# Routing's parts moved within and between chunks, one-hots by scalar per partition, and the last copies of x on GpSimd, in an mLSTM, mixture-of-experts and MLP kernel

## The chip, the cores and the metric

The kernel runs on one core of a Trainium2 chip. The metric is the device time of one execution in microseconds (us), as the median of some runs. The engines are TensorE (PE; its weight loads are listed as PEld), VectorE (DVE), ScalarE (ACT), GpSimd (POOL) and the queue of SyncE (SP), which issues most of the transfers.

## The reference

Three stages in a row: an mLSTM attention over 768 steps, 2 x 8 heads of 40; a mixture of 8 experts in which each of 1536 tokens takes its two best; and an MLP.

```python
def _attn_ref(q, k, v, i_gate, f_gate, o_gate):
    for t in range(S):
        m_new = np.maximum(f_gate[:, :, t] + m, i_gate[:, :, t])
        f_stab = np.exp(f_gate[:, :, t] + m - m_new)
        i_stab = np.exp(i_gate[:, :, t] - m_new)
        C = f_stab * C + i_stab * einsum('bhd,bhe->bhde', vt, kt)
        n = f_stab * n + i_stab * kt
        y[:, :, t] = o * einsum('bhde,bhe->bhd', C, qt) / max(|n.q|, 1)

def _moe_ref(x, w_gate, w_noise, noise, w1, w2):
    noisy_logits = x @ w_gate + log1p(exp(x @ w_noise)) * noise
    top2 = np.argpartition(-noisy_logits, 2, axis=1)[:, :2]
    top2_w = softmax of the two
    for e in range(E):
        out[mask] += top2_w[mask] * (relu(x[mask] @ w1[e]) @ w2[e])

def _moe2_ref(x, w_in, w_out):
    h = x @ w_in
    return (h * clip(h + 3, 0, 6) / 6) @ w_out
```

## The kernel before

**Attention.** The 768 steps are cut into NT = 12 chunks of 64 for both batches (128 partitions: 2 batches x 64 steps). The loop at L1137 runs chunks n = 0 to 9; chunks 10 and 11 are written out behind it (L1201 to L1228). In a chunk: `pmul(n+1)` (VectorE: scores times decay), `inter(n)` and `values(n)` (TensorE), `logits(n-2)` (TensorE: the router's logits of an earlier chunk), `norm2(n-1)` (ScalarE: the chunk's x, then the copy of its last 64 columns, and SP's store of x into `Xd`), `state(n)` (TensorE, then VectorE's Sb), `norm_eg` and `norm_pv` (VectorE: y, its denominator), `scores(n+2)` and `expo(n+2)` (TensorE, then ScalarE's dd), `xpose(n-1)` (TensorE transposes x, ScalarE copies xT), and parts of the weights' split: `w_load` (SP loads a piece into one of four buffers `raw`), `w_hi` (ScalarE casts its high part) and `w_lo` (VectorE subtracts for the low part). The schedule is by hand: each engine runs its instructions in the order of the program's text.

**Routing.** `route(m)` is a generator for tokens of four chunks (m = 0, 1, 2). Its parts: the logits' copy (L475) and softplus; the two best and one-hots over experts (up to L518); the counting by matmuls on TensorE (L527 to L538); the slot of each token (to L582); one-hots of the slot's low part over 128 columns (LO, L587) and its high part over 32 (H and HV, L592, L595); matmuls that turn these into lists of tokens (L605); `idx` (L608) and the copy of slots (L612); and the shares of the two experts (L617 to L621). Each `yield` ends a step; a `yield` with "D" or "P" ends a part. `go(r)` runs to the next such part; after `fine[0] = True` the function `step()` advances by one `yield` from within the later code, and `until(m)` runs on until list m is found. The logits and lists of all routes, and half of the output of `values`, lie in PSUM bank 7 (`wb`).

**Experts.** `units` are eight experts cut into tiles of up to 416 tokens, with experts 0 and 1 begun on the tokens of the first eight chunks (units 0 and 1) and finished later (units 2 and 8). For each unit `gather` (GpSimd, indirect) fetches tokens from `Xd` by `idx`, `xprep` transposes them on TensorE and ScalarE and VectorE split them into XH and XL; a step f runs `L1` (TensorE, then hb on ScalarE and VectorE), and `L2` two steps later (LAG). `bg(i, f, fn)` puts a piece of other work at step f of unit i, behind its matmuls, `bga` ahead of the L2; WS lists at which steps `w_split` (`w_hi`, `w_lo`, `w_load`) runs.

**MLP.** Units M0 = 9 and later are the MLP. `conv` converts its float64 weights in pieces of six parts on VectorE, ScalarE (L748) and SP; `combine` joins the two experts' rows by the shares.

Of the kernel before, what the change touches and what calls it, by code (L numbers as in the profile page):

```python
# [11 lines left out]
F32 = mybir.dt.float32  # L12
# [13 lines left out]
NT = 12  # L26
# [18 lines left out]
R4 = 4  # L45
XP = (2, 3, 5, 6)
VSPLIT = {}
WS = ((0, 0), (0, 1), (0, 3), (0, 5), (0, 7), (1, 1), (1, 2), (1, 4), (1, 6), (2, 1))
# [24 lines left out]
def mlstm_moe_mlp(ctx, tc, qk, kv, on, gf, gf4, sl, w1, w2, w_in, w_out, cf, cb, out):  # L73
# [329 lines left out]
    def norm2(n):  # L403
# [9 lines left out]
        A.copy(x[:, DM:XW], x[:, 256:DM])  # L413
        xt[n] = x
        nc.sync.dma_start(Xd[n * 128:(n + 1) * 128], x)
# [40 lines left out]
    found, now = [0], [False]  # L456
# [14 lines left out]
    def route(m):  # L471
# [48 lines left out]
        e2 = small([128, R4, 1], "e2")  # L520
# [13 lines left out]
        A.activation(e2, dl, AF.Exp)  # L534
# [46 lines left out]
        lf = small([128, 2, 2 * R4], "lf", F16)  # L581
# [3 lines left out]
        for i in (0, R4):  # L585
            LO.append(scratch(R4, 128))
            V.tensor_tensor(LO[-1], iotab[:, None, :].to_broadcast([128, R4, 128]),  # L587
                            lf[:, 0, i:i + R4, None].to_broadcast([128, R4, 128]), OP.is_equal)
            yield
        hh = wp.tile([128, DM], F32, name="yo2", bufs=1).bitcast(F16)  # L590
        H, HV = [hh[:, i:i + 64 * R4].rearrange("p (j c) -> p j c", c=32) for i in (0, 64 * R4)]
        V.tensor_tensor(H, iotab[:, None, 0:32].to_broadcast([128, 2 * R4, 32]),  # L592
                        lf[:, 1, :, None].to_broadcast([128, 2 * R4, 32]), OP.is_equal)
        yield
        V.tensor_tensor(HV.rearrange("p (n k) c -> p n k c", n=R4), H.rearrange("p (n k) c -> p n k c", n=R4),  # L595
                        tokf[:, tks, None, None].to_broadcast([128, R4, 2, 32]), OP.mult)
# [4 lines left out]
        while fine[0] and spot[0] < at + SPI and not now[0]:  # L601
            yield
        pi = pz[:, 128:160]
# [12 lines left out]
        sm = small([128, R4, 1], "s")  # L616
        V.tensor_scalar(sm, e2, 1.0, 1e-9, OP.add, OP.add)  # L617
        yield
        V.reciprocal(wab[:, :, 0:1], sm)
        yield  # L620
        V.tensor_tensor(wab[:, :, 1:2], wab[:, :, 0:1], e2, OP.mult)  # L621
        yield
# [509 lines left out]
    def norm(n):  # L1132
        norm_pv(n)
        norm2(n)

    L = NT - 3
    for n in range(NT - 2):  # L1137
# [13 lines left out]
        if n in (7, 9):  # L1151
            go(r0)
# [5 lines left out]
        if n > 1:  # L1158
            norm2(n - 1)
        if n and n % 2 == 0:  # L1160
            gate(n, 2)
# [10 lines left out]
        if n >= 5:  # L1172
            go(r0)
# [10 lines left out]
        scores(n + 2)  # L1184
# [248 lines left out]
```

## Time and profile before

| | us |
|---|---|
| median of 3 runs | 508.97 |
| lowest, highest | 506.79, 509.3 |
| the profiled execution | 510.91 |
| its span, first to last instruction | 509.1 |

| engine | busy us | share of the span |
|---|---|---|
| TensorE, matmuls | 478.2 | 94% |
| TensorE, weight loads | 436.5 | 86% |
| VectorE | 332.4 | 65% |
| ScalarE | 238.5 | 47% |
| GpSimd | 96.4 | 19% |

The attention stage runs to about 98 us, the experts to about 324, the MLP to the end. A row of the timeline gives start, duration, engine, line, operation, output and inputs, shape and count; what stands in brackets is how long the engine was idle before it and what ended that. [...] The shares of busy time are means over stages with different limits.

### The profile page before, as it was taken

The numbers are of one execution on the slowest core, as the hardware profiler recorded it, in microseconds if no ns is written. First come the engines' busy times: TensorE is split into PE (matmuls) and PEld (weight loads), VectorE is DVE, ScalarE is ACT, GpSimd is POOL, SyncE is SP. The second block draws the span as 40 slices with busy tenths as digits, with TensorE's granted clock in tenths as the row PEclk, the third lists the DMA queues.
The fourth block names the chain that finished last, engine by engine and source line by source line (L and its number), as shares of the span: only waits on it lengthen the run. The fifth ranks groups of instructions, "written<-read, shape, count | busy, mean of one in ns | idle before, by whom it ended". The sixth has DMA issues, their size and how long they took to land. (4 is left out here: it accounts for less than half of the span.)

```text
span 509.1 us, 11544 instructions
## 1 busy us (share of the span) xinstructions
PE 478.2 (94%) x4554; PEld 436.5 (86%) x4554; DVE 332.4 (65%) x823; ACT 238.5 (47%) x509; POOL 96.4 (19%) x115
## 2 busy tenths in 40 slices
PE   6898887799999999999999999899999999999996
PEld 3676665698899999999999999789888989899985
DVE  4844788588648788887878774577886334353534
ACT  3576568265435454545455633556463324233331
POOL 2322211503231111111110021785101000000000
PEclk9999995599999999999999999999999999999999
DMA  8597672555755798979797696869313400020111
GB/s 208 161 298 188 199 225 102 145 178 169 263 180 193 245 301 273 310 258 312 264 311 245 215 308 196 280 189 327 135 53 108 151 1 1 1 52 1 26 26 52
DMA packets 41192, 91.00 MB, mean 179 GB/s; under 512 B 4816, under 2 KB 23504, under 8 KB 41136
## 3 DMA queue, kind: packets, MB, share of 16 engines
q1 hardware_dynamic: 34736, 69.52, 43.0%
q0 software_dynamic: 5728, 19.73, 12.8%
q10 hardware_dynamic: 672, 0.99, 0.7%
q8 instruction: 36, 0.59, 0.5%
q14 instruction: 20, 0.16, 0.1%
HBM read 67.42 MB, written 22.68 MB: 177 GB/s over the span
## 5 line engine op out<-in xcount | busy, mean ns | idle before, releaser
L952 DVE SCALAR_TENSOR_TENSOR r<-r,bank 128x512 f32<-128x512 f32 (+1 forms) x56 | 34.2, 611 | 82.0 <-ACT r L951 78.9
L951 ACT ACTIVATE r<-bank,cft 128x512 f32<-128x512 f32 (+1 forms) x56 | 35.1, 627 | 96.9 <-PE bank L937 88.3
L940 ACT ACTIVATE hb<-bank 128x416 fp32r<-128x416 f32 (+2 forms) x80 | 35.7, 447 | 88.5 <-PE bank L937 75.6
L937 PE MATMUL bank<-XH,SB 128*128 128x416 f32 (+3 forms) x280 | 75.8, 341 | 0.3 <-PEq L1037 0.3
L937 PE MATMUL bank<-XL,SB 128*128 128x416 f32 (+3 forms) x192 | 67.0, 349 | 0.6 <-DVE XL L876 0.6
L973 PE MATMUL bank<-SB,hb 128*128 128x320 f32 x192 | 61.9, 322 | 2.4 <-ACT hb L924 2.1
L973 PE MATMUL bank<-SA,hb 128*128 128x320 f32 x192 | 60.8, 317 | 0.0
L864 POOL DMA_INDIRECT XG<-Xd,idx x32 | 34.6, 1081 | 138.2 <-PE bank L874 110.2
L975 PE MATMUL bank<-SA,hb 128*128 128x320 f32 x192 | 59.4, 309 | 0.1
L975 PE MATMUL bank<-SB,hb 128*128 128x320 f32 x192 | 59.5, 310 | 0.0
L974 PE MATMUL bank<-SA,hb 128*128 128x320 f32 x192 | 59.2, 308 | 0.0
L974 PE MATMUL bank<-SB,hb 128*128 128x320 f32 x192 | 59.2, 308 | 0.0
L937 PEld LDWEIGHTS bank<-XH,SB 128*128 128x128 f32 x280 | 50.3, 189 | 4.6 <-issue 0.6
L937 PE MATMUL bank<-XH,SA 128*128 128x416 f32 (+2 forms) x200 | 50.9, 327 | 0.0
L973 PEld LDWEIGHTS bank<-SB,hb 128*128 128x128 f32 x192 | 36.2, 188 | 3.9 <-ACT hb L924 2.5
L937 PE MATMUL bank<-XL,SA 128*128 128x416 f32 (+2 forms) x120 | 39.0, 326 | 0.0
L937 PEld LDWEIGHTS bank<-XL,SB 128*128 128x128 f32 x192 | 36.2, 188 | 2.8 <-DVE XL L876 0.8
L937 PEld LDWEIGHTS bank<-XH,SA 128*128 128x128 f32 x200 | 36.2, 194 | 1.4
L973 PEld LDWEIGHTS bank<-SA,hb 128*128 128x128 f32 x192 | 36.1, 188 | 1.1
L974 PEld LDWEIGHTS bank<-SA,hb 128*128 128x128 f32 x192 | 36.2, 188 | 0.9
L974 PEld LDWEIGHTS bank<-SB,hb 128*128 128x128 f32 x192 | 36.2, 189 | 0.6
L975 PEld LDWEIGHTS bank<-SA,hb 128*128 128x128 f32 x192 | 36.0, 188 | 0.6 <-DVE hb L925 0.3
(215 smaller groups left out, 1038.9 us busy)
## 6 DMA issues: line engine op xcount, KB each, us to landing
raw<-in_w_dram SPq DMA_DIRECT2D x18, 640.0 KB
raw<-in_w_dram SPq DMA_DIRECT2D x18, 512.0 KB
craw<-in_w_in_dram SPq DMA_DIRECT2D x8, 640.0 KB
craw<-in_w_out_dram SPq DMA_DIRECT2D x8, 640.0 KB
raw<-in_w_dram SPq DMA_DIRECT2D x18, 256.0 KB
qk<-in_qk_dram SPq DMA_DIRECT2D x23, 192.0 KB
Yd<-yo SPq DMA_DIRECT2D x24, 160.0 KB
kv<-in_kv_dram SPq DMA_DIRECT2D x11, 324.0 KB
```

Of the source, the lines that this page charges most:

```text
L864: G.indirect_dma_start(out=XG[0:n, (u.xo + i) % 4, :], out_offset=None, in_=Xd[0:CUT[u.i] * 128] if early else Xd[:, :], in_offset=bass.In ...
L937: T.matmul(p, a, b, start=(i == 0), stop=(i == 7))
L940: A.activation(hb[:, 0:N], p, AF.Relu)
L951: A.activation(r, p, AF.Relu, bias=three)
L952: V.scalar_tensor_tensor(r, r, 6.0, p, OP.min, OP.mult)
L973: T.matmul(p, h, wh, start=s, stop=False)
L974: T.matmul(p, h, wl, start=False, stop=False)
L975: T.matmul(p, hb[:, lo:lo + n], wh, start=False, stop=t)
```

## The change

The calls `go(r0)` of chunks 5 to 9 go from behind `norm_pv` to the end of the chunk, and the counting of route 0 from ahead of `logits` in chunk 7 to behind `scores`. The one-hots over the slot are made by 16 VectorE instructions, each with one column of `lf` (now float32) as a scalar per partition, in place of three that broadcast and one that multiplies; their `yield`s are two more for LO and one more for HV. The exponential for the shares goes ahead of the list's matmuls. The shares are put aside and run at steps 2, 4 and 6 of unit 1. The store of x is a function of its own, `put`, called behind `norm2`. The copy of x's last 64 columns runs on GpSimd for chunks 10 and 11. One `w_lo` and `w_load` goes from ahead of unit 0 into it; WS has other steps; list 2 and the gather of unit 2 are asked for at step 1 of unit 1, not 2; and `conv` runs at the odd steps of unit M0, not the even ones.

```diff
--- before.py
+++ after.py
@@ -45,7 +45,7 @@
 R4 = 4
 XP = (2, 3, 5, 6)
 VSPLIT = {}
-WS = ((0, 0), (0, 1), (0, 3), (0, 5), (0, 7), (1, 1), (1, 2), (1, 4), (1, 6), (2, 1))
+WS = ((0, 2), (0, 3), (0, 4), (0, 5), (0, 7), (1, 2), (1, 3), (1, 4), (1, 6), (2, 1))
 TROWS = CAP + 11 * 128
 OVB = 22
 OV = OVB * 128
@@ -410,9 +410,11 @@
         else:
             G.tensor_tensor(x[:, 0:DM].rearrange("p (a x d) -> p x a d", a=4, x=2), o.rearrange("p (x a) d -> p x a d", x=2),
                             rd.rearrange("p (x a) -> p x a", x=2)[:, :, :, None].to_broadcast([128, 2, 4, D]), OP.mult)
-        A.copy(x[:, DM:XW], x[:, 256:DM])
+        (A.copy if n < NT - 2 else G.tensor_copy)(x[:, DM:XW], x[:, 256:DM])
         xt[n] = x
-        nc.sync.dma_start(Xd[n * 128:(n + 1) * 128], x)
+
+    def put(n):
+        nc.sync.dma_start(Xd[n * 128:(n + 1) * 128], xt[n])
 
 
     Xd = dram.tile([SLOTS, XW], F32, name="Xd")
@@ -453,7 +455,7 @@
                 r = slice(32 * c, 32 * c + 32)
                 T.matmul(p[r], xT[n][0:w, k, r], wgt[0:w, k, :], start=(k == 0), stop=(k == 2))
 
-    found, now = [0], [False]
+    found, now, shares = [0], [False], []
 
     def until(m):
         now[0] = True
@@ -517,7 +519,7 @@
         dl = small([128, R4, 1], "dl")
         V.tensor_tensor(dl, mx[:, :, 1:2], mx[:, :, 0:1], OP.subtract)
         wab = WAB[:, tks]
-        e2 = small([128, R4, 1], "e2")
+        e2 = small([128, R4, 1], "e2", bufs=3)
         if not fine[0]:
             yield "P"
             assert counted[0] >= m
@@ -531,7 +533,6 @@
                      mk[:, i:i + 1].to_broadcast([128, k, 8]), start=False, stop=False, skip_group_check=True)
         T.matmul(pp.rearrange("p (n e) -> p n e", n=R4), ones, run[:, None, :].to_broadcast([128, R4, 8]),
                  start=False, stop=True, skip_group_check=True)
-        A.activation(e2, dl, AF.Exp)
         cuts = [e for e in range(2) if m == CUT[e] // R4]
         if m == 1 or cuts:
             pc = pz[:, 96:104]
@@ -578,28 +579,29 @@
         yield
         V.scalar_tensor_tensor(lh[:, 1], sli, 7, h1, OP.bitwise_and, OP.bitwise_or)
         yield
-        lf = small([128, 2, 2 * R4], "lf", F16)
+        lf = small([128, 2, 2 * R4], "lf")
         V.tensor_copy(lf, lh)
         yield "D" if not fine[0] else None
         LO = []
-        for i in (0, R4):
-            LO.append(scratch(R4, 128))
-            V.tensor_tensor(LO[-1], iotab[:, None, :].to_broadcast([128, R4, 128]),
-                            lf[:, 0, i:i + R4, None].to_broadcast([128, R4, 128]), OP.is_equal)
-            yield
-        hh = wp.tile([128, DM], F32, name="yo2", bufs=1).bitcast(F16)
-        H, HV = [hh[:, i:i + 64 * R4].rearrange("p (j c) -> p j c", c=32) for i in (0, 64 * R4)]
-        V.tensor_tensor(H, iotab[:, None, 0:32].to_broadcast([128, 2 * R4, 32]),
-                        lf[:, 1, :, None].to_broadcast([128, 2 * R4, 32]), OP.is_equal)
-        yield
-        V.tensor_tensor(HV.rearrange("p (n k) c -> p n k c", n=R4), H.rearrange("p (n k) c -> p n k c", n=R4),
-                        tokf[:, tks, None, None].to_broadcast([128, R4, 2, 32]), OP.mult)
+        for j in range(2 * R4):
+            if j % R4 == 0:
+                LO.append(scratch(R4, 128))
+            V.tensor_scalar(LO[-1][:, j % R4], iotab, lf[:, 0, j:j + 1], None, OP.is_equal)
+            if j % 2:
+                yield
+        HV = wp.tile([128, DM], F32, name="yo2", bufs=1).bitcast(F16)[:, 0:64 * R4].rearrange("p (j c) -> p j c", c=32)
+        for j in range(2 * R4):
+            n = R4 * m + j // 2
+            V.tensor_scalar(HV[:, j], iotab[:, 0:32], lf[:, 1, j:j + 1], tokf[:, n:n + 1], OP.is_equal, OP.mult)
+            if j % 4 == 3:
+                yield
         at = spot[0]
         yield
         if not fine[0]:
             yield "P"
         while fine[0] and spot[0] < at + SPI and not now[0]:
             yield
+        A.activation(e2, dl, AF.Exp)
         pi = pz[:, 128:160]
         for j in range(2 * R4):
             T.matmul(pi, LO[j // R4][:, j % R4], HV[:, j], start=(j == 0), stop=(j == 2 * R4 - 1))
@@ -613,13 +615,14 @@
         elif m == 1:
             V.tensor_tensor(slot, slot, pi, OP.add)
         yield
-        sm = small([128, R4, 1], "s")
-        V.tensor_scalar(sm, e2, 1.0, 1e-9, OP.add, OP.add)
-        yield
-        V.reciprocal(wab[:, :, 0:1], sm)
-        yield
-        V.tensor_tensor(wab[:, :, 1:2], wab[:, :, 0:1], e2, OP.mult)
-        yield
+
+        def share():
+            sm = small([128, R4, 1], "s")
+            V.tensor_scalar(sm, e2, 1.0, 1e-9, OP.add, OP.add)
+            V.reciprocal(wab[:, :, 0:1], sm)
+            V.tensor_tensor(wab[:, :, 1:2], wab[:, :, 0:1], e2, OP.mult)
+
+        shares.append(share)
         if m == NT // R4 - 1:
             at = spot[0]
             while spot[0] < at + SP2:
@@ -1132,6 +1135,8 @@
     def norm(n):
         norm_pv(n)
         norm2(n)
+        if n:
+            put(n)
 
     L = NT - 3
     for n in range(NT - 2):
@@ -1148,7 +1153,7 @@
             load_kv(n + 3)
         if n in (0, 1, 3, 5, 7):
             load_on(n + 2 + n % 2 if n else 2)
-        if n in (7, 9):
+        if n == 9:
             go(r0)
         if n >= 2 and n != L:
             logits(n - 2)
@@ -1157,6 +1162,8 @@
             gens.append(r0)
         if n > 1:
             norm2(n - 1)
+        if n:
+            put(n - 1)
         if n and n % 2 == 0:
             gate(n, 2)
         state(n)
@@ -1169,8 +1176,6 @@
         if n == 1:
             G.tensor_copy(adj, iota8)
             G.tensor_copy(iotab, iota128)
-        if n >= 5:
-            go(r0)
         for _ in range(WD[n] if n < len(WD) else 0):
             w_load()
         if n == 0:
@@ -1182,6 +1187,8 @@
         if n == L - 1:
             xpose(n - 1)
         scores(n + 2)
+        if n == 7:
+            go(r0)
         if n == L - 1:
             logits(n - 1)
             r1 = [route(1), "D"]
@@ -1196,6 +1203,8 @@
             decays(n + 2, n + 6)
         if 1 <= n < L - 1:
             xpose(n - 1)
+        if n >= 5:
+            go(r0)
         w_hi(WH[n] if n < len(WH) else 0)
         w_lo(WL[n] if n < len(WL) else 0)
     n = NT - 2
@@ -1207,6 +1216,7 @@
     xpose(n - 2)
     go(r1)
     norm2(n - 1)
+    put(n - 1)
     state(n)
     logits(n - 2)
     fine[0] = True
@@ -1218,8 +1228,6 @@
     norm(n)
     norm_eg(n + 1)
     norm(n + 1)
-    w_lo()
-    w_load()
     open_psd()
     xprep(units[0], 0, 5)
     xpose(n - 1, 2)
@@ -1270,8 +1278,11 @@
     bga(0, 1, last_route)
     bg(0, 0, gather, units[1])
     bg(0, 1, open_late)
-    bg(0, 0, w_lo)
-    bg(0, 0, w_load)
+    for f in range(2):
+        bg(0, f, w_lo)
+        bg(0, f, w_load)
+    for f in (2, 4, 6):
+        bg(1, f, lambda: shares.pop(0)())
     for f in range(8):
         bg(0, f, step, 6 if f < 4 else 4)
     for f in range(3):
@@ -1279,8 +1290,8 @@
     for i, f, *c in WS:
         for g_ in {'h': (w_hi,), 'l': (w_lo, w_load)}[c[0]] if c else (w_split,):
             bg(i, f, g_)
-    bg(1, 2, until, NT // R4)
-    bg(1, 2, gather, units[2])
+    bg(1, 1, until, NT // R4)
+    bg(1, 1, gather, units[2])
     bg(1, 4, gather, units[3], 0, 1)
     bg(1, 7, gather, units[3], 2, 3)
     for i in range(3, M0 - 1):
@@ -1300,7 +1311,7 @@
     bg(M0 - 2, 3, conv_to, 4)
     bg(M0 - 2, 7, conv_to, 8)
     for f in range(8):
-        bg(M0, 2 * f, conv)
+        bg(M0, 2 * f + 1, conv)
         bg(M0 + 1, f, conv, 2)
     bg(M0, 7, conv_to, 12)
     bg(M0 + 1, 7, conv_to, 16)
```

## Rows read from the trace of the kernel before

**Rows 1.** Windows of 10 us: per engine busy us (instructions), granted clock, DMA share, GB/s.

```profile
80.00:90.00 10.00, 6.25 (x188) 5.50 (x187) 9.32 (x38) 6.59 (x18) 1.81 (x2) 0.50 0.38 142
...
110.00:120.00 10.00, 9.44 (x76) 9.03 (x75) 9.76 (x34) 5.33 (x11) 0.00 (x0) 1.00 0.43 142
...
130.00:140.00 10.00, 10.00 (x81) 9.78 (x79) 6.06 (x23) 4.49 (x9) 1.41 (x2) 1.00 0.73 233
```

**Rows 2.** Timeline of TensorE, `values` (L365): start us, us, engine line op tile shape count.

```profile
39.70 1.07 PE L365 MATMUL bank<-kv,P 64*64 64x41 f32 x32
...
68.47 0.66 PE L365 MATMUL bank<-kv,P 64*64 64x41 f32 x32
...
84.20 1.07 PE L365 MATMUL bank<-kv,P 64*64 64x41 f32 x32
```

**Rows 3.** Timeline, waits of chunks 5 to 9; in brackets idle before and releaser.

```profile
56.47 0.65 PE L454 MATMUL bank<-cft,xT 128*32 128x16 f32 x24 [1.19 <-ACT xT L441]
...
63.84 0.21 ACT L534 ACTIVATE e<-dl 128x4 f32<-128x4 f32 x1 [1.40 <-DVE dl L518]
...
75.80 1.09 PE L365 MATMUL bank<-kv,P 64*64 64x41 f32 x30 [1.24 <-DVE zg L475]
...
77.05 0.69 DVE L317 TENSOR_TENSOR P<-s4p,dd 128x512 f32<-128x512 f32 x1 [1.30 <-ACT dd L305]
...
83.09 0.18 PE L527 MATMUL bank<-mk,cbt 128*128 128x32 bf16 x1 [3.06 <-DVE slot L612]
```

**Rows 4.** Timeline of VectorE: three small operations, the one-hots of route 0, the shares.

```profile
69.88 0.17 DVE L576 TENSOR_SCALAR lh<-SL 128x8 int32<-128x8 int32 x1
...
69.96 0.16 DVE L577 TENSOR_SCALAR h<-SL 128x8 int32<-128x8 int32 x1
...
70.16 0.17 DVE L579 SCALAR_TENSOR_TENSOR lh<-SL,h 128x8 int32<-128x8 int32 x1
...
73.57 1.24 DVE L587 TENSOR_TENSOR yo<-iotab,lf 128x512 f16<-128x512 f16 x2
...
74.73 0.42 DVE L592 TENSOR_TENSOR yo<-iotab,lf 128x256 f16<-128x256 f16 x1
...
75.19 0.42 DVE L595 TENSOR_TENSOR yo<-yo,cft 128x256 f16<-128x256 f16 x1
...
82.95 0.16 DVE L617 TENSOR_SCALAR s<-e 128x4 f32<-128x4 f32 x1
...
83.44 0.15 DVE L542 TENSOR_SCALAR t<-bank 128x1 f32<-128x1 f32 x1
```

**Rows 5.** Timeline around the end of the attention stage, 91 to 99 us.

```profile
91.33 0.73 POOL L411 TENSOR_TENSOR x<-od,rd 128x320 f32<-128x320 f32 x1
...
94.05 1.44 DVE L688 TENSOR_TENSOR SA<-raw,SA 128x1280 fp32r<-128x1280 f32 x1
...
94.28 1.79 POOL L411 TENSOR_TENSOR x<-od,rd 128x320 f32<-128x320 f32 x1 [2.21 <-DVE rd L399]
...
96.10 0.24 ACT L413 COPY x<-x 128x64 f32<-128x64 f32 x1 [3.76 <-POOL x L411]
...
97.05 0.65 PE L454 MATMUL bank<-cft,xT 128*32 128x16 f32 x24 [2.67 <-ACT xT L441]
...
98.19 0.56 PE L937 MATMUL bank<-XH,SA 128*128 128x256 f32 x1
```

**Rows 6.** Timeline of units 0 and 1: a split, and waits.

```profile
101.04 1.48 DVE L688 TENSOR_TENSOR SA<-raw,SA 128x1280 fp32r<-128x1280 f32 x1
...
106.71 1.23 DVE L688 TENSOR_TENSOR SB<-raw,SB 128x1024 fp32r<-128x1024 f32 x1 [1.02 <-ACT SB L687]
...
116.36 0.39 PE L937 MATMUL bank<-XL,SB 128*128 128x256 f32 x1 [0.56 <-DVE XL L876]
...
128.79 0.52 PE L874 MATMUL bank<-cft,XG 128*128 128x128 f32 x3 [1.19 <-DMA XG<-Xd,idx]
```

**Rows 7.** Timeline of TensorE in the transition to unit M0.

```profile
328.17 0.41 PE L973 MATMUL bank<-SB,hb 128*128 128x320 f32 x1 [1.02 <-ACT hb L924]
```

## The prediction

> **What bounds the kernel now.** I read the windows of 10 us first, to see where TensorE is not full: from 130 us on it is busy for 10.00 of 10, so whatever is gained or lost before that is carried to the end, apart from the waits in the transition near 328 us [rows 1, 7]. Every edit but one (the conversion's) lies before 135 us. In 80 to 90 TensorE is busy 6.25 of 10 and VectorE 9.32; in 110 to 120 VectorE is busy 9.76 [rows 1]. So the path runs through VectorE at the end of the attention stage and nearly so in unit 0.
>
> Next the clock. The granted clock reads 1.00 at 40 us and 0.50 at 84 us, but the same 32 matmuls of `values` take 1.07 us in both and 0.66 us at 68 us [rows 2]. [...] The sum below therefore prices the stage at the long durations.
>
> Then the waits in time order. TensorE stands 1.24 us before `values(9)` for VectorE's copy of the logits (L475), and 3.06 us before route 1's counting (L527) for the copy of slots (L612) [rows 3]. In the code neither pair shares data: they share PSUM bank 7 (`wb`), so I read it that a write waits for all earlier reads of the bank in program order. This I use below for the new order.
>
> **Routing's parts at the end of a chunk (n = 5 to 9).** `go(r0)` goes behind `scores`, `expo` and `xpose`. VectorE's order changes only in chunks 8 and 9; ScalarE's and TensorE's change in all.
> Chunk 5: ScalarE no longer stands before the gates, dd(7) and xT(4) until VectorE delivers the logits; TensorE's 1.19 us wait for xT [rows 3] goes. Chunk 7: the counting of route 0 (L527 to L532) now stands behind `scores(9)` and ahead of `expo(9)`. By bank 7 it must wait until VectorE has read y of chunk 7; behind it stand `expo(9)`, and for that dd(9) on ScalarE and the product on VectorE. No row has this wait. It can cost nothing, if VectorE has read by then, and at most the 1.19 us that chunk 5 gained, since with those lost chunk 7 stands as before; I take 1.0, since VectorE was the later of the two in this chunk. ScalarE's wait of 1.40 us for `dl` [rows 3] goes, as the exponential of `dl` moves to the counting's next part, where `dl` is long done. Net at the state update of chunk 8: 0 to 1.2 us gained; I take 0.2.
> Chunk 8: the logits' copy now comes ahead of route 0's one-hots on VectorE. So ScalarE's softplus and dd(10) no longer sit behind them, and the 1.30 us that VectorE waits for dd(10) [rows 3] goes: 1.3. The one-hots themselves stay on VectorE's path ahead of pmul(10).
> Chunk 9: the copy of slots comes behind route 1's counting, so the wait of 3.06 falls. It isn't worth 3.06, because VectorE is the fuller engine; late next is bank 7's next reader, the y of chunk 9. The three operations on the shares (82.95 to 83.44) leave VectorE: 0.5 [rows 4]. They return in unit 1 at steps 2, 4 and 6, beside a full TensorE.
> Sum until route 1's list of tokens: 0.2 + 1.3 + 0.5 = **2.0 us** (1.4, if dd(10) comes 0.4 later than VectorE is ready, to 3.0).
>
> **Copies of x on GpSimd, and w_lo moved.** For chunks 10 and 11 ScalarE's copy of 64 columns stands in ScalarE's queue waiting 3.76 us for GpSimd's x; behind it stand the casts of the gathered tokens and xT(9), and TensorE waits 2.67 us for that [rows 5]. GpSimd's x(11) itself took 1.79 us beside VectorE's split L688 (94.05), against 0.73 us for x(10) [rows 5]. After: ScalarE can cast as soon as the transposes are done. TensorE's wait ended at 97.05, so it began at 94.4; unit 0's first matmul came 1.14 after the logits (98.19) [rows 5], so 95.6 on the old time scale. Late next is VectorE's XL of the second tile, at about the same time, and then the gather's landing. I take **2.2 us** (1.5 to 2.6). GpSimd's two copies cost no more than x itself (0.73) each; they stand ahead of the second gather (needed 15 us later) and of the store of x, so nothing is charged; without that cover 0.3 to 1.5. SP's queue keeps its order: each store (`put`) is issued where it was, and the weight loads stay behind it.
>
> **Splits in unit 0.** Two w_lo (1.48 us each [rows 6]) now come at steps 0 and 1, and splits at steps 2, 3, 4, 5, 7 instead of 0, 1, 3, 5, 7. Between step 1's hb and unit 1's XL VectorE gets one w_lo and one split more: 1.48 + 1.2 = 2.7 us, against idle time there of at least 1.02 [rows 6] which it fills. TensorE waits for XL 0.56 us now [rows 6]; it will wait longer by about 1.1, and is repaid when unit 1's step 1 has no split any more. I take **-0.5** (-2.7 to 0). Weights: every piece of WS is still split at least four steps ahead of its first use and its load, from the same four buffers, asked for four or more steps ahead of its cast; nothing is charged.
>
> **Gather of unit 2 at step 1.** In GpSimd's queue nothing else stands there, so the issue doesn't move by the edit itself; but the split that ran beside it goes to step 2. TensorE's 1.19 us wait for its landing [rows 6] shrinks: **+0.6** (0 to 1.2).
>
> **Conversion at odd steps of unit M0.** TensorE waits 1.02 us at 328 for ScalarE's hb [rows 7]; in the code the conversion's L748 of step 0 stands ahead of it on ScalarE. One step later it stands ahead of the next hb, behind `combine`. From one side the wait goes (+1.0), from the other a second one of its size arises (-1.0). I take **0**.
>
> **One-hots.** Before: from 73.57 to 75.61, 2.04 us for a route [rows 4]. After: eight instructions of 128 columns and eight of 32. None of this form is in the trace. From below: two independent small VectorE instructions start 0.08 apart, so 16 x 0.08 = 1.3. From above: each behind the other, 0.20 for 8 columns and 0.46 for 256 (74.73 to 75.19), so about 0.33 for 128 and 0.22 for 32: 8 x 0.33 + 8 x 0.22 = 4.4 [rows 4]. They don't depend on one another, so I stay near the lower row: 0.12 each, 1.9 us, **+0.2** for the two routes on the path (-4.7 to +1.5; the third lies in unit 0, where VectorE has little room).
> [...]
>
> **Sum.** 2.0 + 2.2 - 0.5 + 0.6 + 0 + 0.2 = 4.5 us. The profiled execution took 510.91 us (span 509.1), so 506.4 by its own time. It lies 1.94 us above the median of the three runs, 508.97; on that scale the forecast is **504.5 us**. A difference of 0.5% (2.5 us) is about what a measurement of this kernel can tell from none.
>
> **Rivals.**
> *VectorE keeps the gain in unit 0.* For: 9.76 of 10 busy there already. Against: it idles 1.02 at 105.7, and TensorE waited only 0.56. Price: -2.7 instead of -0.5 and no shorter gather wait: 4.5 - 2.2 - 0.6 = 1.7, so 507.3.
> *Costly one-hots (slower).* If each waits for the one before, a route pays 4.4 instead of 2.04, three routes 7.1, and 4.3 + 0 - 7.1 = -2.8: 511.8. It decides from a mean of 0.22 us an instruction (2.04 + 4.3/3 over 16: no gain left), and 0.27 makes it slower by over 0.5%. Against: the pair 0.08 apart.
> [...]
> *It doesn't do what it says.* Bank 7 holds the moved counting just as long, and the gathered tile lands too late for ScalarE's freed queue to matter: only the 0.5 us of the shares is left, 508.5.
>
> **How the numbers follow.** Forecast 0.50 (nearly all of it under 506.4), earlier clock or cheap one-hots 0.15, VectorE in unit 0 0.22, no effect 0.05, costly one-hots 0.08. Faster: 0.50 + 0.15 less a little for the forecast's upper edge, 0.64; same 0.28; slower 0.08. The range: with the one-hots at their middle the terms' lower ends sum to -0.6 (1.4 + 1.5 - 2.7 + 0 - 1.0 + 0.2) and their upper ends with cheap one-hots to 9.3 (3.0 + 2.6 + 0 + 1.2 + 1.0 + 1.5). That all meet at one end is unlikely; 500 to 509.5 leaves out the costly one-hots and little else.
>
> **What would show it.** Right: no wait of ScalarE for GpSimd's x; `values(9)` and L527 without their waits; VectorE busy throughout from 75 to the list of tokens, and that list 1.4 to 2.8 us earlier; unit 0's first L1 3.5 to 5 us earlier; sixteen one-hots in about 1.9 us; TensorE's wait before unit 1's first L1 longer than 0.56 and the gather's wait shorter than 1.19. Wrong: one-hots of over 0.2 us each; a new TensorE wait of over 2 us for XL or hb in unit 0; the lead at unit 0's start gone by 130 us; or a new stall in unit M0.

## The result and the profile after

The changed kernel took 503.84 us (median of 4 runs, 502.13 to 504.99) against 509.13 for the kernel before (506.79 to 510.53): a ratio of 0.9898, interval 0.9849 to 0.9947. The forecast was 504.5. Run again on another chip, beside the kernel before, it took 507.58 against 510.85: 0.9948, interval 0.9924 to 0.9971. By these medians the change is worth some 3 to 5 us. The total came out as forecast, but by luck: two large errors in the sum cancelled, as the stretches show.

The profiled execution of the changed kernel took 504.61 us, its span 502.8. Its windows (columns as in [rows 1], which they answer):

```profile
80.00:90.00 10.00, 8.15 (x201) 6.51 (x200) 9.38 (x48) 3.36 (x14) 2.40 (x3) 0.50 0.34 122
...
110.00:120.00 10.00, 7.91 (x59) 6.89 (x59) 9.79 (x39) 3.57 (x7) 0.96 (x1) 1.00 0.48 112
130.00:140.00 10.00, 10.00 (x84) 9.85 (x83) 5.77 (x25) 4.48 (x11) 0.03 (x1) 1.00 0.89 273
```

VectorE is as full as before in both critical windows (9.38, 9.79), TensorE is fuller in 80 to 90 and emptier in 110 to 120, and from 130 us on it is full again. (The changed kernel is some 2 us further on in its work in the first of these windows and 4 to 5 in the second, so equal windows don't hold equal work.)

One pair of profiles doesn't tell a change of 1% from chance, so I set the stretches of all profiles side by side. Marks: Sb(n) is the start of VectorE's Sb of chunk n, "list 1" that of idx of route 1, "unit 0" the first L1, "unit 1, 160" the first L1 of 160 columns. "Changed" are the profiles, those of the experiments below among them, whose code in that stretch is that of the changed kernel: six up to list 1, four to unit 0, three in each of the last two.

| stretch | before, two profiles | changed, lowest to highest (mean) | gain | forecast |
|---|---|---|---|---|
| start to Sb(4) | 42.20, 41.37 | 39.50 to 44.35 (40.95) | 0.8 | 0 |
| Sb(4) to Sb(5) | 8.64, 8.64 | 4.63 to 7.49 (6.53) | 2.1 | 0 |
| Sb(5) to Sb(7) | 14.68, 14.58 | 13.09 to 14.76 (14.00) | 0.6 | 1.2 |
| Sb(7) to Sb(8) | 5.52, 5.86 | 6.95 to 6.96 (6.96) | -1.3 | -1.0 |
| Sb(8) to list 1 | 17.43, 17.43 | 17.70 to 17.72 (17.71) | -0.3 | 2.0 |
| list 1 to unit 0 | 9.72, 8.79 | 6.87 to 6.99 (6.92) | 2.3 | 2.2 |
| unit 0 to unit 1, 160 | 36.00, 36.68 | 35.26 to 35.91 (35.60) | 0.7 | 0.1 |
| from there to the end | 374.91, 373.45 | 373.47 to 376.29 (374.48) | -0.3 | 0 |

A gain is the mean of before less that of changed; before rounding they add up to 4.8 us. Of the 4.4 forecast between Sb(5) and unit 0, the routing's 2.2 turned into a loss of 0.9 (0.63 - 1.27 - 0.28); in its place stand 2.9 us from ahead of Sb(5), where I had expected nothing.

Two rows are weaker than they look. Ahead of Sb(5) the other six experiments have the changed kernel's code too. Over all twelve profiles the first row is 39.50 to 44.42 (mean 41.45) and the second 4.63 to 7.54 (6.76), so their gains are 0.3 and 1.9, and the profile of the third experiment reaches Sb(5) at 50.87 us, no earlier than before (50.84, 50.01). In the last row the chip counts: the four profiles on the chip of the second group take 374.99 to 378.53 there, the other profiles of these kernels 373.03 to 374.01.

Single profiles can mislead here. In the profiled execution route 1's list came 1.65 us earlier than before and unit 0's first L1 4.49 earlier, as the prediction's signs ask; but Sb(5) was already 3.42 earlier.

Where the 2.1 between Sb(4) and Sb(5) lie, the timeline of TensorE shows (start us, us, engine line, count, idle time before and what ended it). The kernel before, in its two profiles:

```profile
44.60 1.13 PE L294 MATMUL s4p<-qk 40*64 40x64 f32 x30 [2.31 <-issue]
```

```profile
43.77 1.13 PE L294 MATMUL s4p<-qk 40*64 40x64 f32 x30 [2.31 <-issue]
```

The changed kernel:

```profile
40.41 1.12 PE L294 MATMUL s4p<-qk 40*64 40x64 f32 x30 [0.39 <-issue]
```

"Issue" is a pause for which the profile shows no cause. It is 2.31 us in both profiles of before and at most 1.21 in the twelve of the changed kernel and the experiments.

Now the routing. The timeline of the changed kernel, chunks 7 to 9 (it answers [rows 3, 4]):

```profile
63.72 0.18 PE L529 MATMUL bank<-mk,cbt 128*128 128x32 bf16 x1 [0.78 <-DVE y L386]
...
71.75 1.38 DVE L589 TENSOR_SCALAR yo<-iotab,lf 128x128 f16<-128x128 f16 x8
73.05 2.04 DVE L595 TENSOR_SCALAR yo<-iotab,lf,cft 128x32 f16<-128x32 f16 x7
73.34 0.73 POOL L310 TENSOR_TENSOR kt<-kv,dd 128x320 f32<-128x320 f32 x1 [2.90 <-ACT dd L305]
74.81 0.48 DVE L595 TENSOR_SCALAR yo<-iotab,lf,cft 128x32 f16<-128x32 f16 x2
75.20 0.68 DVE L317 TENSOR_TENSOR P<-s4p,dd 128x512 f32<-128x512 f32 x1
...
80.07 0.18 PE L529 MATMUL bank<-mk,cbt 128*128 128x32 bf16 x1 [1.82 <-DVE y L386]
83.53 1.38 DVE L589 TENSOR_SCALAR yo<-iotab,lf 128x128 f16<-128x128 f16 x8
84.83 1.67 DVE L595 TENSOR_SCALAR yo<-iotab,lf,cft 128x32 f16<-128x32 f16 x8
```

The rows come from two views that meet at 75 us, so one of route 0's eight instructions of 32 columns stands in both. The one-hots of route 0 take from 71.75 to 75.29, 3.5 us, and those of route 1 from 83.53 to 86.50, 3.0, where four instructions took 2.04 [rows 4]. The product for the next chunk (L317) starts as soon as they end: they are on the path. VectorE no longer waits for dd(10); TensorE's counting now waits for bank 7's reader y (0.78 and 1.82) and not for the slots.

Route 0 takes longer than route 1 because of one instruction, here alone:

```profile
73.24 0.86 DVE L595 TENSOR_SCALAR yo<-iotab,lf,cft 128x32 f16<-128x32 f16 x1
```

The others of its kind took 0.28 us. It ran beside GpSimd's product L310 (73.34 to 74.07). In the kernel before, that product came behind the one-hots of 73.57 to 75.61:

```profile
77.09 0.74 POOL L310 TENSOR_TENSOR kt<-kv,dd 128x320 f32<-128x320 f32 x1 [4.74 <-ACT dd L305]
```

It waits for dd(10), which the new order makes earlier, and so it now falls among the one-hots. The experiments on the one-hots and on the order bear this out: some 0.6 us of route 0's 3.5 are the price of the new order, not of the new instructions.

The end of the stage (it answers [rows 5]) and unit 0 (it answers [rows 6]):

```profile
90.48 0.88 PE L877 MATMUL bank<-cft,XG 128*128 128x128 f32 x3 [1.58 <-DMA XG<-Xd,idx]
91.39 0.48 ACT L878 CAST XH<-bank 128x384 fp32r<-128x384 f32 x1 [5.10 <-PE bank L877]
91.62 0.72 POOL L411 TENSOR_TENSOR x<-od,rd 128x320 f32<-128x320 f32 x1 [0.62 <-PE bank L441]
93.70 0.56 PE L940 MATMUL bank<-XH,SA 128*128 128x256 f32 x1
...
109.36 1.48 DVE L691 TENSOR_TENSOR SB<-raw,SB 128x1280 fp32r<-128x1280 f32 x1
...
111.44 0.41 DVE L879 TENSOR_TENSOR XL<-bank,XH 128x256 fp32r<-128x256 f32 x1
...
111.90 0.39 PE L940 MATMUL bank<-XL,SB 128*128 128x256 f32 x1 [1.52 <-DVE XL L879]
```

ScalarE casts as soon as TensorE has transposed; its wait for GpSimd's x is gone, and the gather's landing ends last (1.58). At unit 1's start TensorE's wait for XL has grown from 0.56 to 1.52 us. The split of 1.48 ahead of XL (109.36) stood there before as well:

```profile
113.82 1.48 DVE L688 TENSOR_TENSOR SB<-raw,SB 128x1280 fp32r<-128x1280 f32 x1
```

### The profile page after: what moved, and what is told of

Its sections match the earlier page's. It is cut to its first block, busy times and chain, and to the rows that moved or that the text cites. A ratio compares the mean times of both kernels' runs of the same rounds, so it can differ in the third digit from the quotient of the medians.

```text
span 502.8 us, 11581 instructions
## 1 busy us (share of the span) xinstructions
PE 478.6 (95%) x4554; PEld 436.6 (87%) x4554; DVE 335.9 (67%) x859; ACT 238.3 (47%) x507; POOL 96.5 (19%) x117
## 5 line engine op out<-in xcount | busy, mean ns | idle before, releaser
L949 DVE SCALAR_TENSOR_TENSOR hb<-bank,hb 128x32 fp32r<-128x32 f32 x64 | 12.0, 187 | 37.7 <-ACT hb L943 37.6
L976 PEld LDWEIGHTS bank<-SA,hb 128*128 128x128 f32 x192 | 36.1, 188 | 1.1
L977 PEld LDWEIGHTS bank<-SA,hb 128*128 128x128 f32 x192 | 36.2, 188 | 0.9
```

The lines of the kernel that those rows point to most:

```text
L949: V.scalar_tensor_tensor(hb[:, N:N + u.tail], p[:, o:N], 0.0, hb[:, o:N], OP.max, OP.subtract)
L976: T.matmul(p, h, wh, start=s, stop=False)
L977: T.matmul(p, h, wl, start=False, stop=False)
```

## The experiments

Each kernel but the kernel before, run once more, differs from the changed one by the edit shown. Medians are compared only among kernels that ran together on one chip: the first four, the next four, the last four (there the kernel before took 507.87, 510.85 and 507.96).

**The one-hots as before.**

```diff
-        lf = small([128, 2, 2 * R4], "lf")
+        lf = small([128, 2, 2 * R4], "lf", F16)
...
-            V.tensor_scalar(LO[-1][:, j % R4], iotab, lf[:, 0, j:j + 1], None, OP.is_equal)
...
-            V.tensor_scalar(HV[:, j], iotab[:, 0:32], lf[:, 1, j:j + 1], tokf[:, n:n + 1], OP.is_equal, OP.mult)
...
+            V.tensor_tensor(LO[-1], iotab[:, None, :].to_broadcast([128, R4, 128]),
+                            lf[:, 0, i:i + R4, None].to_broadcast([128, R4, 128]), OP.is_equal)
...
+        V.tensor_tensor(H, iotab[:, None, 0:32].to_broadcast([128, 2 * R4, 32]),
+                        lf[:, 1, :, None].to_broadcast([128, 2 * R4, 32]), OP.is_equal)
...
+        V.tensor_tensor(HV.rearrange("p (n k) c -> p n k c", n=R4), H.rearrange("p (n k) c -> p n k c", n=R4),
+                        tokf[:, tks, None, None].to_broadcast([128, R4, 2, 32]), OP.mult)
```

> The changed kernel with the one-hots made as before: four instructions that broadcast, in place of 16 with a scalar per partition. Theory (the one-hots' price lies on VectorE's path): in the changed kernel the 16 took 3.5 us for route 0 and 3.0 for route 1, before 2.0 each, so from the cast of lf in route 1 to idx it takes 3.2 us in place of 3.98, and with 0.9 to 1.5 us back per route the time is 1.5 to 3 us under the changed kernel's 503.8, about 501.5. Rival (bank 7 or TensorE sets the list's time, and the dearer one-hots hide): the one-hots shrink to 2.0 us but the time stays within 1 us of 503.8.

```profile
72.27 1.28 DVE L588 TENSOR_TENSOR yo<-iotab,lf 128x512 f16<-128x512 f16 x2
73.47 0.42 DVE L593 TENSOR_TENSOR yo<-iotab,lf 128x256 f16<-128x256 f16 x1
73.86 0.74 POOL L310 TENSOR_TENSOR kt<-kv,dd 128x320 f32<-128x320 f32 x1 [2.90 <-ACT dd L305]
73.92 0.96 DVE L596 TENSOR_TENSOR yo<-yo,cft 128x256 f16<-128x256 f16 x1
...
84.77 0.42 DVE L596 TENSOR_TENSOR yo<-yo,cft 128x256 f16<-128x256 f16 x1
```

In this timeline route 0 takes 72.27 to 74.88, 2.6 us, route 1 2.1. Route 0's last instruction took 0.96 us beside GpSimd's product, which route 1's (0.42) doesn't meet. From Sb(7) to list 1 it takes 22.97 us against 24.65 to 24.67 in six profiles of the changed code: 1.7 us for two routes. From lf of route 1 to its idx it takes 3.22, as expected. The time was 502.93 us, ratio to before 0.9898 (0.9871 to 0.9925). Beside the next kernel but one, which has all 16 instructions and 504.38, that is 1.5 us less; the intervals of the two overlap, but the stretch shows the gain. The theory holds.

**Only H and HV as before.**

```diff
-            V.tensor_scalar(HV[:, j], iotab[:, 0:32], lf[:, 1, j:j + 1], tokf[:, n:n + 1], OP.is_equal, OP.mult)
...
+        V.tensor_tensor(H, iotab[:, None, 0:32].to_broadcast([128, 2 * R4, 32]),
+                        lf[:, 1, :, None].to_broadcast([128, 2 * R4, 32]), OP.is_equal)
...
+        V.tensor_tensor(HV.rearrange("p (n k) c -> p n k c", n=R4), H.rearrange("p (n k) c -> p n k c", n=R4),
+                        tokf[:, tks, None, None].to_broadcast([128, R4, 2, 32]), OP.mult)
```

> The changed kernel with only the one-hots of the high part (H and HV) made as before; the low part (LO) keeps its eight instructions with one scalar. Theory (the dear half is HV with two scalars: 2.2 and 1.9 us against 0.9 before, while LO took 1.4 against 1.2): nearly as fast as with all one-hots as before, 501.5 to 502. Rival (each of the 16 costs alike, 0.2 us): half of the way, about 502.7, with LO at 1.6 us or more.

502.91 us, ratio 0.9894 (0.9856 to 0.9932); Sb(7) to list 1 takes 23.07 us, 0.1 from the kernel with all as before. LO by scalars costs 1.38 us against 1.28. The dear half is HV.

**The token's number in LO, not in HV.**

```diff
-            V.tensor_scalar(LO[-1][:, j % R4], iotab, lf[:, 0, j:j + 1], None, OP.is_equal)
+            V.tensor_scalar(LO[-1][:, j % R4], iotab, lf[:, 0, j:j + 1], tokf[:, n:n + 1], OP.is_equal, OP.mult)
...
-            V.tensor_scalar(HV[:, j], iotab[:, 0:32], lf[:, 1, j:j + 1], tokf[:, n:n + 1], OP.is_equal, OP.mult)
+            V.tensor_scalar(HV[:, j], iotab[:, 0:32], lf[:, 1, j:j + 1], None, OP.is_equal)
```

> The changed kernel with the token's number multiplied into LO (128 columns, now two scalars) and not into HV (32 columns, now one scalar); the lists come out the same. Theory (the second scalar is what costs): LO's instructions now stand 0.28 us apart in place of 0.17, HV's 0.17 in place of 0.21 to 0.28. Rival (the price is that of 32 columns, or of a following instruction): LO stays at 0.17 and HV at 0.21 to 0.28. The time stays within 1 us of the changed kernel's 503.8 by both.

```profile
85.26 1.87 DVE L590 TENSOR_SCALAR yo<-iotab,lf,cft 128x128 f16<-128x128 f16 x8
87.04 1.19 DVE L595 TENSOR_SCALAR yo<-iotab,lf 128x32 f16<-128x32 f16 x8
```

Start to start, an instruction of LO takes (87.04 - 85.26) / 8 = 0.22 us with two scalars, against (84.83 - 83.53) / 8 = 0.16 with one in the changed kernel. The run of HV ends with the duration of its last instruction (0.22 and 0.29), so one of HV takes (1.19 - 0.22) / 7 = 0.14 with one and (1.67 - 0.29) / 7 = 0.20 with two. So the price hangs on the number of scalars per partition and hardly on the columns. The theory holds, with 0.22 where 0.28 was named. From Sb(7) to list 1 it takes 24.60 us, as changed; the time was 504.38 (0.9918).

**The last copies of x on ScalarE again.**

```diff
-        (A.copy if n < NT - 2 else G.tensor_copy)(x[:, DM:XW], x[:, 256:DM])
+        A.copy(x[:, DM:XW], x[:, 256:DM])
```

> The changed kernel with the last copies of x (chunks 10 and 11) back on ScalarE; the w_lo stays in unit 0. From idx of route 1 to unit 0's first L1 it took 9.7 us before and 6.9 changed. Theory (the copies in ScalarE's queue carry that gain): ScalarE waits some 2 to 4 us for GpSimd's x again, the stretch takes 8.5 to 9.5 us, and the time is about 2 us above the changed kernel, 505.8. Rival (the w_lo that no longer stands ahead of unit 0 carries it): the stretch stays under 7.5 us and the time at 503.8.

```profile
89.47 0.24 ACT L413 COPY x<-x 128x64 f32<-128x64 f32 x1 [4.13 <-POOL x L411]
91.31 0.24 ACT L413 COPY x<-x 128x64 f32<-128x64 f32 x1 [1.60 <-POOL x L411]
```

ScalarE's waits are back in its timeline, but list 1 to unit 0 takes only 7.53 us, 0.6 more than changed: the theory's 8.5 to 9.5 is wrong, and the rival's bound of 7.5 is just missed. 505.45 us (0.9953, 0.9925 to 0.998) is 1.1 over the kernel ahead of it, with intervals that overlap.

**The changed kernel again.** No edit.

> The changed kernel once more, beside the others. Theory (what lies ahead of the logits' copy of route 0 differs from execution to execution and isn't the change's): that copy may start anywhere from 49 to 54 us, while from there to idx of route 1 it takes 35.2 to 36.9 us and from idx to unit 0's first L1 6.9. Rival (the change itself makes the start earlier): the copy starts within 0.5 us of 49.9 again. The time is 503 to 505 by both.

The logits' copy of route 0 starts at 49.40, so this profile alone bears out the rival; but the six profiles of the same code start it between 48.91 and 51.46, against 53.31 and 52.48 before. Most of that difference is the pause ahead of L294. Still, the theory is right that the place isn't fixed: the third experiment, whose code is the same up to there, starts the copy at 53.34. The time was 507.58, over the 503 to 505 named, as was that of the kernel before on this chip. The clock's rise moves too: the granted clock goes from 0.50 to 1.00 at 102 us in the first profile of before and at 96 in that of the changed kernel. By durations, the first L1 of 0.28 or 0.29 us (0.41 at the lower clock) comes 4.0 and 3.9 us behind unit 0's first L1 in the profiles of before, and 0.3 to 3.3 behind it in the four of the changed code, so part of the 0.7 us gained in units 0 and 1 is likely the clock's.

**The old order of chunks 5 to 9.**

```diff
-        if n == 9:
+        if n in (7, 9):
             go(r0)
         if n >= 2 and n != L:
             logits(n - 2)
...
+        if n >= 5:
+            go(r0)
         for _ in range(WD[n] if n < len(WD) else 0):
             w_load()
...
         scores(n + 2)
-        if n == 7:
-            go(r0)
...
             xpose(n - 1)
-        if n >= 5:
-            go(r0)
         w_hi(WH[n] if n < len(WH) else 0)
```

> The changed kernel with the calls of routing in chunks 5 to 9 where they were before (behind norm_pv, and ahead of logits in chunk 7); all else changed. Theory (the order gives the attention stage's gain): from the logits' copy of route 0 to idx of route 1 it takes 1.5 to 3 us more than the 35.2 to 36.9 us of the changed kernel, ScalarE's and TensorE's waits of chunk 5 (1.19 us) and VectorE's for dd(10) (1.30 us) are back, and the time is about 2 us above the changed kernel. Rival (VectorE's work sets the stretch whatever the order, and only the shares' removal counted): the stretch stays within 0.7 us and the time too.

```profile
53.28 0.65 PE L456 MATMUL bank<-cft,xT 128*32 128x16 f32 x24 [0.98 <-ACT xT L443]
...
71.63 1.67 DVE L595 TENSOR_SCALAR yo<-iotab,lf,cft 128x32 f16<-128x32 f16 x8
73.48 1.08 PE L365 MATMUL bank<-kv,P 64*64 64x41 f32 x30 [1.75 <-DVE zg L477]
74.73 0.69 DVE L317 TENSOR_TENSOR P<-s4p,dd 128x512 f32<-128x512 f32 x1 [1.30 <-ACT dd L305]
74.78 0.74 POOL L310 TENSOR_TENSOR kt<-kv,dd 128x320 f32<-128x320 f32 x1 [5.62 <-ACT dd L305]
...
80.77 0.19 PE L529 MATMUL bank<-mk,cbt 128*128 128x32 bf16 x1 [3.05 <-DVE slot L614]
```

Four of the five waits of [rows 3] are back in the timeline: 0.98 us for 1.19, 1.75 for 1.24, 1.30 for 1.30 and 3.05 for 3.06. (ScalarE's 1.40 for dl isn't: the exponential keeps its new place in this kernel.) GpSimd's product comes behind the one-hots again, and route 0's eight of HV take 1.67 us, as route 1's do in the changed kernel, and not 2.24 (73.05 to 75.29). By stretches, against the lowest of the changed code: Sb(5) to Sb(6) 7.13 (5.86), Sb(6) to Sb(7) 7.54 (7.22), Sb(7) to Sb(8) 5.52 (6.95), Sb(8) to Sb(9) 10.27 (9.41), Sb(9) to list 1 8.78 (8.29). The new order is worth 1.27 + 0.32 - 1.43 + 0.86 + 0.49 = 1.5 us at best; from Sb(5) to list 1 by the mean of the six profiles it is 39.24 - 38.66 = 0.6 us. In three of the six profiles of the changed code an issue pause of 0.57 to 0.63 us falls between Sb(6) and Sb(7), which then takes 8.1; there little is left. The parts behind Sb(7) cancel: with the old one-hots in both, Sb(7) to list 1 takes 22.97 us in the new order and 22.95 and 23.29 in the kernel before. From the logits' copy of route 0 to idx of route 1 it takes 36.77 us against 35.28 to 36.95 in those six: the theory's 1.5 against the lowest, nothing against the highest. The time was 509.09 (0.9975, 0.9952 to 0.9998) against 507.58, 1.5 more, with intervals that overlap. So I call the order's gain likely, not certain.

**One w_lo ahead of unit 0 again.**

```diff
+    w_lo()
+    w_load()
     open_psd()
...
-    for f in range(2):
-        bg(0, f, w_lo)
-        bg(0, f, w_load)
+    bg(0, 0, w_lo)
+    bg(0, 0, w_load)
```

> The changed kernel with one w_lo and w_load back ahead of unit 0 (and one left at its step 0); the last copies of x stay on GpSimd. From idx of route 1 to unit 0's first L1: 9.7 us before, 6.9 changed, 7.5 with the copies back on ScalarE. Theory (the w_lo carries the rest of that gain, since it lies on VectorE and slows GpSimd's x beside it): the stretch takes 8.5 to 9.2 us, GpSimd's x of chunk 11 takes over 1.2 us in place of 0.72, and the time is 1 to 2 us above the changed kernel. Rival (either edit alone is enough, since the gather's landing comes last): the stretch stays under 7.6 us and the time as changed.

```profile
91.58 1.44 DVE L691 TENSOR_TENSOR SA<-raw,SA 128x1280 fp32r<-128x1280 f32 x1
...
91.81 1.79 POOL L411 TENSOR_TENSOR x<-od,rd 128x320 f32<-128x320 f32 x1 [1.85 <-DVE rd L399]
...
93.93 0.58 PE L940 MATMUL bank<-XL,SA 128*128 128x256 f32 x1 [0.35 <-DVE XL L879]
```

GpSimd's x takes 1.79 us beside the split again, as before [rows 5], against 0.72 without it. But list 1 to unit 0 takes 6.91 us: no loss. The rival holds up to that mark: the copies on GpSimd alone bring the whole gain, the w_lo alone all but 0.6. Right behind the mark there is a loss: unit 0's second L1 comes 0.92 us behind the first and waits for XL, where in the changed kernel it comes 0.36 behind it. 507.45 us against 507.58.

**The old one-hots, and unit 0's split of step 5 at step 6.** The one-hots as in the first experiment, and:

```diff
-WS = ((0, 2), (0, 3), (0, 4), (0, 5), (0, 7), (1, 2), (1, 3), (1, 4), (1, 6), (2, 1))
+WS = ((0, 2), (0, 3), (0, 4), (0, 6), (0, 7), (1, 2), (1, 3), (1, 4), (1, 6), (2, 1))
```

> The changed kernel with the one-hots as before, and the split of unit 0's step 5 at step 6. Theory (that split of 1.48 us stands on VectorE ahead of the second tile's XL, for which TensorE waits 1.5 us at unit 1's start): the wait falls under 0.3 us and the time is about 1 us under the 502.9 of the kernel with the old one-hots. Rival (VectorE is full in unit 0, so the wait only moves on to the next thing that VectorE delivers, hb, the copy of yo or the list of route 2): as much waiting stands behind it, and the time stays within 0.5 us of 502.9.

```profile
107.98 0.41 DVE L879 TENSOR_TENSOR XL<-bank,XH 128x256 fp32r<-128x256 f32 x1
...
108.45 0.38 PE L940 MATMUL bank<-XL,SB 128*128 128x256 f32 x1
...
109.26 1.49 DVE L691 TENSOR_TENSOR SB<-raw,SB 128x1280 fp32r<-128x1280 f32 x1
...
113.13 0.35 PE L607 MATMUL bank<-yo,yo 128*128 128x32 f16 x8 [0.54 <-DVE yo L596]
```

TensorE's wait for XL is gone: XL is made ahead of the split now. A wait of 0.54 for the one-hots of route 2 stands in for a third of it. Unit 0 to unit 1, 160 takes 33.97 us, the shortest of all, against 34.92 with the old one-hots alone. Not all of this 0.95 need be the split's, since TensorE's first L1 of 0.28 us comes 0.9 us behind unit 0 here and 3.1 there. An estimate from profiles with a like rise: 35.26 - 33.97 = 1.29 us against the changed kernel run again (0.3 us), of which the old one-hots bring 35.63 - 34.92 = 0.71 (3.0 and 3.1 us), so some 0.6 is left for the split. Behind that mark this profile takes 378.53 us, the longest of all. The kernel took 505.44 us, 2.1 less than the changed kernel on the same chip, and 0.9890 (0.9862 to 0.9918) of the kernel before against 0.9948 (0.9924 to 0.9971): faster than both. How much of the 2.1 is the split's the medians can't tell: the old one-hots alone ran on another chip, at a ratio of 0.9898.

**The kernel before again.**

> The kernel before once more, for a second profile of it. [...]

```profile
52.97 0.66 PE L365 MATMUL bank<-kv,P 64*64 64x41 f32 x32
...
67.95 1.07 PE L365 MATMUL bank<-kv,P 64*64 64x41 f32 x32
```

The short group comes at 53 us here and at 68 in the first profile [rows 2], so the short duration (0.66 us for 1.07) has no fixed place. Yet from the logits' copy of route 0 to idx of route 1 it takes 35.40 us, close to the first profile's 35.16, since the short time saves only 5.86 - 5.52 = 0.3 us in Sb(7) to Sb(8). One profile and one time of 508.57 us.

**The conversion at even steps.**

```diff
-        bg(M0, 2 * f + 1, conv)
+        bg(M0, 2 * f, conv)
```

> The changed kernel with conv at the even steps of unit M0, as before. Theory (a piece of conv only moves from ahead of one hb to ahead of another; forecast 0): TensorE's waits for hb between 315 and 345 us sum to as much as in the changed kernel (0.87 to 1.8 us) and the time is within 0.5 us. Rival (the odd steps took a wait away): two waits of about 1.0 us for hb as before, and about 1 us more.

One wait of TensorE for hb stands between 315 and 345 us, 1.03 us at 324.40, against 0.87 in the changed kernel and 0.86 and 0.94 in its second profile. The kernel before has two in one of its profiles (1.02 and 1.04) and one in the other (1.02). The stretch to the end takes 373.03. So a second wait comes and goes with either code: the theory holds, and the edit is worth nothing that can be seen. 504.76 us (0.9926, 0.99 to 0.9952).

**List 2 and the gather of unit 2 at step 2.**

```diff
-    bg(1, 1, until, NT // R4)
-    bg(1, 1, gather, units[2])
+    bg(1, 2, until, NT // R4)
+    bg(1, 2, gather, units[2])
```

> The changed kernel with list 2 and the gather of unit 2 asked for at step 2 of unit 1, as before. Theory (the earlier request made unit 2's tokens land in time, forecast 0.6 and by the traces 1.2): TensorE's wait of about 1.2 us for the gathered tokens in unit 1 is back and the time is 1 us longer. Rival (they land in time anyway, the list being ready long before step 2): no wait over 0.3, and the time as changed.

```profile
121.86 0.49 PE L877 MATMUL bank<-cft,XG 128*128 128x128 f32 x3
```

No wait: the tokens land in time at step 2 as well, and the rival holds. The step of the request moves nothing: list 2's idx comes 24.5 us behind unit 0's first L1 here, 24.8 and 24.2 in the changed kernel.

The reason that the prediction named isn't the request, though, but the split that ran beside the issue, and this edit leaves the splits where the changed kernel has them. The traces show that reason at work. The issue of the gather's first half, in the kernel before, in the changed one and here:

```profile
122.56 1.77 POOL L864 DMA_INDIRECT XG<-Xd,idx  x1 [18.54 <-DVE s L617]
```

```profile
118.98 0.96 POOL L867 DMA_INDIRECT XG<-Xd,idx  x1 [20.08 <-DVE idx L610]
```

```profile
116.88 0.96 POOL L867 DMA_INDIRECT XG<-Xd,idx  x1 [20.09 <-DVE idx L610]
```

It took 1.77 us in both profiles of before, where a split of 1.22 us had begun 0.3 us ahead of it, and 0.96 or 0.97 in the twelve others, where the split begins 0.5 us behind its start. That is up to 0.8 us of the 1.19 and 1.59 that TensorE waited; no run tests the splits' steps alone. The landing varies besides: with the early request, an issue of 0.96 and H and HV as before the profile has a wait of 1.69 us for the tokens. 505.67 us (0.9953, 0.9925 to 0.9981), with no wait to explain a difference from the kernels beside it.

**The shares made at once.**

```diff
-        shares.append(share)
+        share()
+        yield
...
-    for f in (2, 4, 6):
-        bg(1, f, lambda: shares.pop(0)())
```

> The changed kernel with the shares made in routing, right behind the slots, and not put off to unit 1. Theory (three operations that stand on VectorE's path, forecast 0.5 us): from the cast of lf of route 0 to that of route 1 it takes 0.5 us more than the 15.9 us of the changed kernel, and the time is 0.5 us longer. Rival (they fall into VectorE's waits): within 0.1 us, and no difference in time.

Sb(9) to list 1 takes 8.78 us against 8.29 to 8.30 in six profiles: 0.5, as forecast. From lf of route 0 to that of route 1 it is 16.38. With the old order the same stretch takes 8.78 without the shares; they count only where the order has taken the wait for the slots away. 505.86 us (0.9955, 0.9931 to 0.9978).

## Why the prediction came out, step by step

**Right total, wrong in two places.** The forecast sum was 4.5 us, and the stretches give 4.8; but the one-hots' term is off by 1.9 and the order's by 0.5 or more, while 2.9 us (2.2 by all twelve profiles) come from where the sum has none. That the total came out is luck.

**What bounds the kernel: right.** The long durations hold through most of the stage in the changed kernel too: nine of the eleven groups of 32 matmuls of `values` from 17 to 89 us take 1.07 us, and the granted clock reads 0.50 in each 10 us from 20 to 90. VectorE stays the fuller engine (9.38 of 10 against TensorE's 8.15 in 80 to 90, 9.79 against 7.91 in 110 to 120), which is why each 0.1 us of it counts.

**Routing's order, 2.0: right in mechanism, 1.5 at best, 0.6 on the mean.** Chunk 5 gained up to 1.3, chunk 7 lost 1.1 to 1.4 where 1.0 was taken (the wait for bank 7's reader is there), chunk 8, where dd(10)'s wait went, gave 0.9 for 1.3, the shares 0.5. The sum didn't ask what the earlier dd(10) would set off: GpSimd's product, which waits for it, now runs beside route 0's one-hots and holds one of them up by 0.6 us. "Late next is y of chunk 9" shows as the 1.82 us wait at 80.07.

**One-hots, +0.2: wrong, -1.7.** The failed step is the price of 0.12 us an instruction, "near the lower row". That row is a pair 0.08 apart whose scalars are constants [rows 4]; the new instructions, with one scalar read per partition, start 0.14 to 0.16 apart, and with a second one 0.20 to 0.22. The step from one to two is shown; that the first scalar also makes the step from 0.08 isn't tested, since that pair has int32 and 8 columns. So 16 took 3.0 us, and 3.5 beside GpSimd's product, not 1.9. I had argued from dependence alone and from the number of columns. The rival "costly one-hots" named a break-even at a mean of 0.22; route 1's is 2.97 / 16 = 0.19. Its price of 4.4 a route was too high, and so the total's sign held.

**Copies on GpSimd and the w_lo, 2.2: right in size (2.3).** The gather's landing is late next (1.58), which the prediction named behind the second tile's XL. Either edit is enough for nearly all of it, so the two are no sum.

**Unit 0, -0.5 and +0.6 for the gather: right in mechanism.** The wait for XL grew by 0.96 where 1.1 was said. The wait for the gather (1.19, 1.59) went; the request's new step did nothing, and what the traces show is the reason named, the issue that no longer begins beside a split (0.96 for 1.77), though no run tests it alone. The net gain of 0.7 against 0.1 is likely in part the clock's earlier rise. What the prediction didn't see is that the split of step 5, which stands ahead of XL in both kernels, holds up TensorE: moved behind XL, it took the wait away.

**Conversion, 0: right in size.** Neither of its two sides shows: the wait stays at its place (0.87 for 1.02), and a second one is there in one profile of the changed kernel (0.94) and not in the other.

**What the sum lacked.** The pause of 2.31 us ahead of L294 is in both profiles of before and in none of the others; the stretch from Sb(4) to Sb(5) follows it (8.64 us with 2.31, 7.54 with 1.21, 4.63 to 7.49 with less). The old order, the old one-hots, the old copies, each alone, don't bring it back (0 to 1.21). In the text only the store of x(0) changes its place in a queue ahead of Sb(5), from ahead of chunk 1's loads to behind them, though the prediction has SP's queue keep its order; that wasn't tried, and the cause stays open. So does the 0.8 us ahead of Sb(4) (0.3 by all twelve profiles), which lies within the spread.

## What to carry to other kernels

Price an instruction by a row of its own form: here a second scalar per partition cost 0.06 us an instruction (0.16 to 0.22 on 128 columns, 0.14 to 0.20 on 32), 96 more columns 0.02. If no row has the form, let the sum rest on the dearer neighbour. Where an edit makes one thing earlier, ask what waits for it and beside what that will then run. Where two edits take the same wait away, don't add them; name what is late next, and give it once. Before a total is taken as proof of a sum, compare stretches between marks in several profiles, the ones ahead of the change first.

## What was not expected of the hardware

A VectorE instruction on 128 or 32 columns of float16 took 0.14 to 0.16 us with one scalar per partition and 0.20 to 0.22 with two, start to start (the changed kernel and the third experiment).

VectorE's product of 256 columns took 0.42 us alone and 0.96 beside GpSimd's product of 0.74 us (first experiment), which began 0.06 us earlier; an instruction of 32 columns took 0.86 for 0.28 beside it in the changed kernel. GpSimd's x took 1.79 us beside a split, with one w_lo ahead of unit 0 again, for 0.72 in the changed kernel. So VectorE lost 0.54 us where GpSimd's product ran on for 0.68, and GpSimd 1.07 where the split ran on for 1.21; what slows the one beside the other no run shows.

TensorE's pause of "issue" ahead of L294 was the same 2.31 us in two executions of the kernel before, the same 0.39 in two of the changed kernel, 1.21 in the two programs with H and HV as before and no other change, and smaller in the others: it seems to belong to the program more than to the execution.
